# Softmax of short key rows: the mask added by TensorE, one maximum per PSUM bank, and one shared ring for the loads of q, k and v

## The chip, the cores and the metric

The kernel runs on one core of a Trainium2 chip. The metric is the device time of one execution in microseconds (us). A core has TensorE (PE, matmuls; its weight loads are listed as PEld), VectorE (DVE), ScalarE (ACT), GpSimd (POOL) and a queue engine, SyncE (SP), that here issues nearly all transfers; each engine takes its instructions in the order written.

## The reference

Three stages. First, causal attention with a memory term for B=4 batches, H=8 heads, S=576 positions, D=64 (float32):

```python
scores = scale * np.matmul(q, k.transpose(0, 1, 3, 2))
scores = np.where(causal, -1000000000.0, scores)
scores = scores - scores.max(-1, keepdims=True)
a = np.exp(scores)
a /= a.sum(-1, keepdims=True) + 1e-09
local = np.matmul(a, v)
...
return (g * mem_out + (1 - g) * local).astype(np.float32)
```

`mem_out` is `phi(q) @ M_prev` divided by `phi(q) @ z_prev`. Its output, 2304 tokens of 512 values, goes through two feed-forward layers 512 -> 2048 -> 512, the first with softplus, the second with squared ReLU. All eight weight and activation products are wanted at float32 precision, so the kernel splits each operand in a high and a low 16-bit part and uses three matmuls for one.

## The kernel before

The 4 x 576 query rows are cut into 18 chunks of 128 rows: for two batches at a time, chunk 0 of both, chunk 1 of both, and so on, then one chunk made of the last 64 rows of both. A chunk sees `EXT` keys: 128, 256, 384, 512 or 640. Eight of the 18 chunks (four of 128 keys, four of 256) are the short ones, and they come at two places: chunks 0 to 3 at the very start, chunks 9 to 12 in the middle (their scores fall at about 280 to 350 us).

A step of attention (`emit_s`) takes one head, or for the short chunks a group of `G` heads (4 of 128 keys, 2 of 256), so that a step always has 512 key columns there. For each head TensorE writes the scores into one of two PSUM banks (`s_ps[:, h % 2]`), DVE runs one pass over them (line 314: add the mask, scale, write to `p` in SBUF, and accumulate the minimum into `cs`), and ACT takes the exponential from SBUF with that minimum as bias (line 318). `emit_p` then splits the probabilities in two 16-bit parts (ACT line 330, DVE line 331), and a DMA transpose, or TensorE in the first two chunks, turns them for `emit_pv`.

The inputs of a chunk are loaded by `load` into float32 tiles: `rawk`, `rawq` and `rawv` have one buffer each in the pool `att`; `k` of chunk 1 has one more in the pool `stage`. `prep_k` (lines 226, 227), `prep_q` (217 to 220), `prep_v` (234, 235) and `prep_phi` (251 to 257) turn them into 16-bit parts on ACT and DVE. A `rawq` is read by `prep_q` and later by `prep_phi`, and only then is its buffer free for the next chunk's q. Up to nine chunks of prepared keys and values (`KVB = 9`) are kept.

Work of the first feed-forward layer is laid between the steps of attention: `unit_h` (lines 434 to 436, PSUM tile `hps`), `unit_xq` (496 to 498, `xacc`) and `unit_x` (451 to 453, `xps`). Its 32 weight pieces `wst`, 512 KB each, come as int64-packed words through three staging buffers and are converted by `split_piece`: DVE lines 417, 418, 419 and 422, ACT line 421. The first `unit_h` needs the attention output `xn` of chunks 0 and 1 (line 386), since a block has 256 tokens. The order on each engine is made ahead of time by a list scheduler with priorities (`tc.high_priority`); the second layer (lines 717 to 834) comes after all attention.

Of the kernel before, what the change touches and what calls it, by code (L numbers as in the profile page):

```python
# [8 lines left out]
F32 = mybir.dt.float32  # L9
F16 = mybir.dt.float16  # L10
BF16 = mybir.dt.bfloat16
I32 = mybir.dt.int32
I64 = mybir.dt.int64
AF = mybir.ActivationFunctionType
ALU = mybir.AluOpType
AX = mybir.AxisListType

P = 128
# [20 lines left out]
NST = 3  # L39
PTB = 4  # L40
PB = 2
P16 = 2
ST2 = 4

# [2 lines left out]
def kernel(  # L47
# [15 lines left out]
    pe, act, dve, pool, sp = nc.tensor, nc.scalar, nc.vector, nc.gpsimd, nc.sync  # L63
    B, H, S, D = q.shape
# [46 lines left out]
    att = att_cm.__enter__()  # L111
# [4 lines left out]
    stage = stage_cm.__enter__()  # L116


    mask = att.tile([P, 2, 4 * P], BF16, name="mask")
# [15 lines left out]

    p16 = [att.tile([P, 2 * EMAX], F16, name=f"p16_{i}") for i in range(P16)]
    zero = stage.tile([P, P], F16, name="zero", bufs=1)
    ident = stage.tile([P, P], F16, name="ident", bufs=1)
    make_identity(nc, ident)
    dve.memset(zero, 0.0)  # L140
    for t in p16:
        dve.memset(t, 0.0)
    s_ps = sps.tile([P, 2, 512], F32, name="s_ps")
# [16 lines left out]
    raw, qT, phiT, KT, V, Mt, Pt, PT, pvt, cs_t = ({} for _ in range(10))  # L160

    def segs(g):
        x = CH[g]
        if len(x) == 2:
            return [(x[0], P * x[1], 0, P)]
        return [(2 * x[0] + i, 4 * P, i * R, R) for i in range(2)]

    def lo_eng(g):
        return dve if g < LOE else pool

    def load(nm, g, pool_=None):
        if g >= NC or (nm, g) in raw:
            return
        src = {"q": q, "k": k, "v": v}[nm]
        t = (pool_ or att).tile([P, H, D], F32, name="raw" + nm, bufs=1)
        for b, s0, r0, n in segs(g):
            sp.dma_start(out=t[r0:r0 + n], in_=src[b, :, s0:s0 + n, :].rearrange("h p d -> p h d"))
        raw[nm, g] = t
    def load_m(g):
        for b, s0, r0, n in (segs(g) if g < NC else []):  # L180
            if s0 == 0:
                t = att.tile([P, EMAX], F32, tag="Pt", name="mraw", bufs=PB)[:, :HD].rearrange("p (h d) -> p h d", h=H)
                for i in range(2):
# [3 lines left out]
    def transp(g, out, in_, lim):  # L187
        nblk = in_.shape[1] // P
        if g >= lim:
            step = nblk if nblk <= 12 else nblk // 2  # L190
            for a in range(0, nblk, step):
                e = a + step
                sp.dma_start_transpose(out=out[:, a:e], in_=in_[:, a * P:e * P])
            return
        for a in range(0, nblk, 8):
            e = min(nblk, a + 8)
            ps = mm.tile([P, 8, P], F16, tag="mm", name="tps")
            for i in range(a, e):
                pe.transpose(ps[:, i - a], in_[:, i * P:(i + 1) * P], ident)
            act.activation(out[:, a:e], ps[:, :e - a], AF.Copy)  # L200
# [47 lines left out]
    def prep_phi(g):  # L248
        r = raw.pop(("q", g))
        e = att.tile([P, H, D], F32, tag="prod", name="phie")  # L250
        act.activation(e, r, AF.Relu, scale=-1.0)
        act.activation(e, e, AF.Exp, scale=-1.0)
        f = att.tile([P, H, D], F32, name="phi")
        dve.scalar_tensor_tensor(f, r, 0.0, e, ALU.max, ALU.add)
        fn = att.tile([P, H, 2, D], F16, name="phin")
        act.activation(fn[:, :, 0, :], f, AF.Copy)
        lo_eng(g).tensor_tensor(fn[:, :, 1, :], f, fn[:, :, 0, :], ALU.subtract)
        phiT[g] = att.tile([P, H, P], F16, name="phiT", bufs=2)
        transp(g, phiT[g], fn.rearrange("p h t d -> p (h t d)"), TP)
# [18 lines left out]
    def kblocks(g):  # L278
        x = CH[g]
        if len(x) == 2:  # L280
            return [[POS[x[0], i]] for i in range(x[1] + 1)]
        return [[POS[2 * x[0] + j, i] for j in range(2)] for i in range(4)] + [[g]]

    def emit_s(g, h0):
        G, ext = GRP[g], EXT[g]
        p = att.tile([P, EMAX], F32, name="Pt", bufs=PB)
        if h0 == 0:
            cs_t[g] = att.tile([P, 2, H], F32, name="cs", bufs=3)
        cs = cs_t[g]
        mk = mask[:, :, :EMAX // 2] if ext > 512 else mask[:, 0, 4 * P - ext:]  # L290
        for i in range(G):
            h = h0 + i
            pf = p[:, i * ext:(i + 1) * ext]
            if ext <= 512:
                half = ext
                view, pw, mw = s_ps[:, h % 2, :ext], pf, mk
            else:
                half = ext // 2
                view = s_ps[:, :, :half]
                pw, mw = pf.rearrange("p (a c) -> p a c", a=2), mk  # L300
            for j, ks in enumerate(kblocks(g)):
                a, n = j * P, P // len(ks)
                while a < (j + 1) * P:
                    e = min((j + 1) * P, (a // half + 1) * half)
                    bank = a // half if half < ext else h % 2
                    o = s_ps[:, bank, a % half:a % half + e - a]
                    for t in range(2):
                        for x, kb in enumerate(ks):
                            pe.matmul(  # L309
                                o[x * n:(x + 1) * n], qT[g][:, t * H + h, x * n:(x + 1) * n],  # L310
                                KT[kb][:, h, a - j * P:e - j * P], start=(t == 0), stop=(t == 1),
                            )
                    a = e
            dve.tensor_tensor_reduce(  # L314
                out=pw, in0=view, in1=mw, scale=-0.125, scalar=3.0e38,
                op0=ALU.add, op1=ALU.min, accum_out=cs[:, 0, h:h + 1],
            )
            act.activation(  # L318
                pf, pf, AF.Exp, bias=cs[:, 0, h:h + 1], scale=-1.0, accum_out=cs[:, 1, h:h + 1],
            )  # L320
        Pt[g, h0] = p
# [185 lines left out]


    load("k", 0)
    load("q", 0)  # L510
    load("k", 1, stage)
    load("v", 0)
    gates()
    z_setup()
# [5 lines left out]
    def prep_part(g, part):  # L520
        if g >= NC:
            return
        if part == 0:
            prep_k(g)
            load("k", g + 1)
        elif part == 1:
            prep_q(g)
        elif part == 2:
            prep_phi(g)
            load("q", g + 1)  # L530
        elif part == 3:
            prep_v(g)
            load("v", g + 1)
            prep_m(g)
            load_m(g + 1)

    prep_k(0)
    prep_q(0)
    prep_phi(0)
    load("q", 1)  # L540
    prep_v(0)
# [13 lines left out]
    def attn_step(s):  # L555
        if s < len(steps):
            g, h = steps[s]
            G = GRP[g]
            with tc.high_priority(HS):
                emit_s(g, h)  # L560
            nst = H // G
            i = h // G
            for part in range(4):
                if part * nst // 4 == i:
                    prep_part(g + 1, part)
            with tc.high_priority(HP):
                emit_p(g, h)
        for g, h0 in pv_at.get(s, ()):
            for h in range(h0, h0 + GRP[g]):
                with tc.high_priority(HV):  # L570
                    emit_pv(g, h)
                if h % 4 == 3:
                    with tc.high_priority(HXE):
                        emit_x(g, h // 4)
# [311 lines left out]
```

## Time and profile before

| | us |
|---|---|
| median of three runs (all: 976.44, 976.58, 980.92) | 976.58 |
| the profiled execution, its own time | 977.68 |
| span of the profiled execution | 975.9 |
| time around the span (977.68 less 975.9) | 1.78 |

The span is from the first to the last instruction of the core. A row of the profile that names `L314` speaks of line 314 of the kernel; `out<-in` are the program's tile names. Busy shares are of the stretch named; the granted clock (PEclk) is 1.00 at 2.4 GHz and 0.50 at 1.2 GHz.

### The profile page before, as it was taken

To read this page: it belongs to the slowest core of one execution; us is meant where nothing else is said; L and a number is where in the kernel's file an instruction comes from. 1 tells how busy PE (TensorE), PEld (TensorE's weight loads), DVE (VectorE), ACT (ScalarE), POOL (GpSimd) and SP (SyncE) were. 2 spreads that over 40 slices of the span, in tenths; PEclk is the share of its full clock that TensorE was granted. 3 is DMA by queue.
4 is the path that set the end of the run, shared out by engine and by line. 5 is a ranking of instruction groups with operands and counts; after the bars stand their busy time and mean duration, and the time that the engine had idled before them with its cause. 6 is when DMAs were issued, how large, how long until landed. Compare 5 with 4: busy or idle time off the path is not lost.

```text
span 975.9 us, 21791 instructions
## 1 busy us (share of the span) xinstructions
PE 884.2 (91%) x8994; PEld 680.1 (70%) x9012; DVE 668.0 (68%) x1437; ACT 587.2 (60%) x1094; POOL 2.2 (0%) x10
## 2 busy tenths in 40 slices
PE   4345898889998899999999999999999999999998
PEld 3234787778877788888888888544684585486483
DVE  7998998877748677675846499998894075066050
ACT  7765878768649687775937556562274065056051
POOL 0000000000000000000000000000000000000000
PEclk8555999999999999999999999999999999999999
DMA  9999989755699976646554375620000000000000
GB/s 232 224 241 215 214 162 195 118 95 112 99 159 176 160 125 104 104 83 108 94 88 80 64 234 172 211 65 22 22 2 11 33 1 4 30 12 1 33 12 22
DMA packets 283219, 101.05 MB, mean 104 GB/s; under 512 B 248048, under 2 KB 280816, under 8 KB 283120
## 3 DMA queue, kind: packets, MB, share of 16 engines
q1 hardware_dynamic: 282880, 99.65, 51.3%
q8 instruction: 70, 1.15, 0.5%
q14 instruction: 29, 0.24, 0.1%
q10 hardware_dynamic: 240, 0.02, 0.0%
HBM read 48.78 MB, written 4.72 MB: 55 GB/s over the span
## 4 chain that ended last, share of the span: by engine, by line
PE 60%; DMA 16%; DVE 13%; ACT 6%; issue 3%; SPq 1%; ACTq 0%; DVEq 0%
DMA PT<-p 8%; PE ops L829 7%; PE ops L827 6%; PE ops L828 6%; PE h2ps L801 4%; PE h2ps L799 4%; PE h2ps L800 4%; DMA rawq<-in_q_dram 3%; PE xps L452 3%; PE xps L451 3%; PE xps L453 3%; PE s_ps L309 3%; PE pvt L354 2%; PE hps L436 2%; PE hps L435 2%
## 5 line engine op out<-in xcount | busy, mean ns | idle before, releaser
L434 PE MATMUL hps<-x,W 128*128 128x256 f16 x576 | 157.8, 276 | 3.2 <-DVE cc L273 3.0
L435 PE MATMUL hps<-x,W 128*128 128x256 f16 x576 | 158.4, 276 | 1.7 <-ACT x L477 1.7
L436 PE MATMUL hps<-x,W 128*128 128x256 f16 x576 | 158.2, 275 | 0.0
L452 PE MATMUL xps<-g,W 128*128 128x256 f16 x512 | 138.5, 273 | 1.7 <-DVE g L445 1.7
L453 PE MATMUL xps<-g,W 128*128 128x256 f16 x512 | 138.7, 273 | 0.0
L451 PE MATMUL xps<-g,W 128*128 128x256 f16 x512 | 137.5, 273 | 1.1 <-DVE spa L441 0.7
L318 ACT ACTIVATE Pt<-Pt,cs 128x128 f32<-128x128 f32 (+4 forms) x144 | 84.2, 585 | 67.4 <-DVE cs L314 67.4
L309 PE MATMUL s_ps<-KT,qT 128*128 128x128 f16 (+2 forms) x992 | 83.9, 225 | 36.6 <-DVE cs L314 35.9
L829 PE MATMUL ops<-W,gg 128*128 128x512 f16 x288 | 108.5, 379 | 0.9
L827 PE MATMUL ops<-W,gg 128*128 128x512 f16 x288 | 109.2, 379 | 0.1
L828 PE MATMUL ops<-W,gg 128*128 128x512 bf16 x270 | 102.3, 379 | 0.0
L309 PEld LDWEIGHTS <-qT 128*128 128x128 f16 (+1 forms) x992 | 59.8, 105 | 48.5 <-issue 43.7
L331 DVE TENSOR_TENSOR p<-Pt,p 128x512 f16<-128x512 f32 (+2 forms) x104 | 69.3, 667 | 29.6 <-ACT p L330 28.8
L831 ACT ACTIVATE osb<-ops 128x512 f32<-128x512 f32 x18 | 10.8, 597 | 123.4 <-PE ops L829 123.4
L808 DVE TENSOR_TENSOR r<-h2ps,r 128x512 f32<-128x512 f32 (+1 forms) x16 | 10.0, 623 | 108.0 <-PE h2ps L801 107.2
L354 PE MATMUL pvt<-V,PT 128*128 128x64 f16 (+1 forms) x1392 | 60.7, 197 | 19.5 <-DMA PT<-p 18.3
L314 DVE CUSTOM_DVE_ANT_0 Pt<-s_ps,mask 128x128 f32<-128x128 f32 (+3 forms) x128 | 62.0, 485 | 18.6 <-PE s_ps L309 17.9
L354 PEld LDWEIGHTS <-PT 128*128 128x128 f16 (+1 forms) x1392 | 50.3, 104 | 28.7 <-DMA PT<-p 25.1
L330 ACT ACTIVATE p<-Pt 128x512 f16<-128x512 f32 (+2 forms) x104 | 63.1, 606 | 11.2 <-DMA PT<-p 10.2
L435 PEld LDWEIGHTS <-W 128*128 128x128 f16 x576 | 56.9, 99 | 10.2 <-issue 3.6
L799 PE MATMUL h2ps<-XT,WS 128*128 128x256 f16 (+1 forms) x256 | 63.7, 259 | 0.0
L800 PE MATMUL h2ps<-XT,WS 128*128 128x256 f16 (+1 forms) x256 | 63.7, 259 | 0.0
(160 smaller groups left out, 2076.5 us busy)
## 6 DMA issues: line engine op xcount, KB each, us to landing
wst<-in_moe_w_in_dram SPq DMA_DIRECT2D x32, 512.0 KB, 5.0
wst<-in_moe_w_out_dram SPq DMA_DIRECT2D x32, 512.0 KB, 4.7
rawk<-in_k_dram SPq DMA_DIRECT2D x16, 256.0 KB, 4.3
rawq<-in_q_dram SPq DMA_DIRECT2D x16, 256.0 KB, 3.9
rawv<-in_v_dram SPq DMA_DIRECT2D x16, 256.0 KB, 4.7
out_dram<-osb SPq DMA_DIRECT2D x16, 256.0 KB, 2.0
PT<-p SPq DMA_TRANSPOSE x100, 3.4
mraw<-in_M_prev_dram SPq DMA_DIRECT2D x8, 128.0 KB, 3.7
```

Of the source, the lines that this page charges most:

```text
L309: pe.matmul(o[x * n:(x + 1) * n], qT[g][:, t * H + h, x * n:(x + 1) * n], KT[kb][:, h, a - j * P:e - j * P], start=(t == 0), stop=(t == 1),)
L354: pe.matmul(o[r], t[:, o0 + i + y, r], V[kb][:, z, h, :], start=(i == 0 and y + z == 0), stop=(i == nb - 1 and y > 0),)
L434: pe.matmul(o, wh, x[:, c], start=(c == 0), stop=False)
L435: pe.matmul(o, wh, x[:, NCC + c], start=False, stop=False)
L436: pe.matmul(o, wl, x[:, c], start=False, stop=(c == NCC - 1))
L451: pe.matmul(ps, wh, gh, start=(f == f0), stop=False)
L452: pe.matmul(ps, wh, gl, start=False, stop=False)
L453: pe.matmul(ps, wl, gh, start=False, stop=(f == f1 - 1))
L799: pe.matmul(o, wh, xh, start=(k == 0), stop=False)
L827: pe.matmul(ps, gh, W4[0][:, f, :], start=(a == 0), stop=False)
L828: pe.matmul(ps, gh, W4[1][:, f, :], start=False, stop=False)
L829: pe.matmul(ps, gl, W4[0][:, f, :], start=False, stop=(a == NFC - 1))
```

## The change

For chunks of up to 256 keys a step now takes one of the two PSUM banks for all its heads (`sb`, the bank alternating by step). TensorE adds the mask of the diagonal block by one more matmul a head (identity `idb` as weights, the 128 x 128 mask as moving operand), DVE takes the maximum over all heads of the bank with one `tensor_reduce` and scales it with a small `tensor_scalar`, and ACT takes each head's exponential from PSUM. Chunks of more keys run the same code as before. Beside it, the loads of q, k and v share one tag of `RAWB = 2` buffers in place of one buffer each (and one in `stage`), and `phi` is computed in place.

```diff
--- before.py
+++ after.py
@@ -39,6 +39,7 @@
 NST = 3
 PTB = 4
 PB = 2
+RAWB = 2
 P16 = 2
 ST2 = 4
 
@@ -138,6 +139,8 @@
     ident = stage.tile([P, P], F16, name="ident", bufs=1)
     make_identity(nc, ident)
     dve.memset(zero, 0.0)
+    idb = att.tile([P, P], BF16, name="idb")
+    act.activation(idb, ident, AF.Copy)
     for t in p16:
         dve.memset(t, 0.0)
     s_ps = sps.tile([P, 2, 512], F32, name="s_ps")
@@ -168,11 +171,11 @@
     def lo_eng(g):
         return dve if g < LOE else pool
 
-    def load(nm, g, pool_=None):
+    def load(nm, g):
         if g >= NC or (nm, g) in raw:
             return
         src = {"q": q, "k": k, "v": v}[nm]
-        t = (pool_ or att).tile([P, H, D], F32, name="raw" + nm, bufs=1)
+        t = att.tile([P, H, D], F32, tag="raw", name="raw" + nm, bufs=RAWB)
         for b, s0, r0, n in segs(g):
             sp.dma_start(out=t[r0:r0 + n], in_=src[b, :, s0:s0 + n, :].rearrange("h p d -> p h d"))
         raw[nm, g] = t
@@ -250,7 +253,7 @@
         e = att.tile([P, H, D], F32, tag="prod", name="phie")
         act.activation(e, r, AF.Relu, scale=-1.0)
         act.activation(e, e, AF.Exp, scale=-1.0)
-        f = att.tile([P, H, D], F32, name="phi")
+        f = e
         dve.scalar_tensor_tensor(f, r, 0.0, e, ALU.max, ALU.add)
         fn = att.tile([P, H, 2, D], F16, name="phin")
         act.activation(fn[:, :, 0, :], f, AF.Copy)
@@ -287,6 +290,28 @@
         if h0 == 0:
             cs_t[g] = att.tile([P, 2, H], F32, name="cs", bufs=3)
         cs = cs_t[g]
+        if G > 1:
+            sb = s_ps[:, h0 // G % 2].rearrange("p (g e) -> p g e", g=G)
+            for i in range(G):
+                h = h0 + i
+                for j, (kb,) in enumerate(kblocks(g)):
+                    o = sb[:, i, j * P:(j + 1) * P]
+                    last = (j + 1) * P == ext
+                    for t in range(2):
+                        pe.matmul(o, qT[g][:, t * H + h], KT[kb][:, h], start=(t == 0), stop=(t == 1 and not last))
+                    if last:
+                        pe.matmul(o, idb, mask[:, 0, 3 * P:], start=False, stop=True)
+            hs = slice(h0, h0 + G)
+            dve.tensor_reduce(cs[:, 0, hs], sb, AX.X, ALU.max)
+            dve.tensor_scalar(cs[:, 0, hs], cs[:, 0, hs], -0.125, None, ALU.mult)
+            for i in range(G):
+                h = h0 + i
+                act.activation(
+                    p[:, i * ext:(i + 1) * ext], sb[:, i], AF.Exp,
+                    bias=cs[:, 0, h:h + 1], scale=0.125, accum_out=cs[:, 1, h:h + 1],
+                )
+            Pt[g, h0] = p
+            return
         mk = mask[:, :, :EMAX // 2] if ext > 512 else mask[:, 0, 4 * P - ext:]
         for i in range(G):
             h = h0 + i
@@ -508,7 +533,7 @@
 
     load("k", 0)
     load("q", 0)
-    load("k", 1, stage)
+    load("k", 1)
     load("v", 0)
     gates()
     z_setup()
```

The scheduler makes a new order of all of it. SP, from its second row, where `raw`, `mraw` and `wst` are the loads of inputs, of the memory matrix and of weight pieces. Before:

```order
L177 DMA rawk<-in_k_dram 128x8x64
L177 DMA rawq<-in_q_dram 128x8x64
L177 DMA rawk<-in_k_dram 128x8x64
L177 DMA rawv<-in_v_dram 128x8x64
L184 DMA mraw<-in_M_prev_dram 64x8x64 x2
L398 DMA wst<-in_moe_w_in_dram 128x4x128 x3
L184 DMA mraw<-in_M_prev_dram 64x8x64 x2
L177 DMA rawq<-in_q_dram 128x8x64
L177 DMA rawk<-in_k_dram 128x8x64
L177 DMA rawv<-in_v_dram 128x8x64
L398 DMA wst<-in_moe_w_in_dram 128x4x128
L401 DMA wst<-in_moe_w_out_dram 128x4x128 x2
```

And now, on the same engine from the same place:

```order
L180 DMA rawk<-in_k_dram 128x8x64
L180 DMA rawq<-in_q_dram 128x8x64
L187 DMA mraw<-in_M_prev_dram 64x8x64 x2
L423 DMA wst<-in_moe_w_in_dram 128x4x128 x3
L180 DMA rawk<-in_k_dram 128x8x64
L187 DMA mraw<-in_M_prev_dram 64x8x64 x2
L180 DMA rawv<-in_v_dram 128x8x64
L423 DMA wst<-in_moe_w_in_dram 128x4x128
L426 DMA wst<-in_moe_w_out_dram 128x4x128
L180 DMA rawq<-in_q_dram 128x8x64
L426 DMA wst<-in_moe_w_out_dram 128x4x128
L180 DMA rawv<-in_v_dram 128x8x64
```

The second k, the first v and what follows moved behind weight pieces; over the first 59 DMA rows the queue issued 18 weight pieces before and issues 23 now.

TensorE, in the scores of chunk 0 (`KT` the keys, `qT` the queries, turned). Before, one matmul of the scores stands here, between transposes (`tps`) and ahead of the first products with the memory matrix:

```order
L199 LDWEIGHTS kn
L199 MATMUL tps<-ident,kn 128x128
L309 LDWEIGHTS qT
L309 MATMUL s_ps<-KT,qT 128x128
L346 LDWEIGHTS phiT
L346 MATMUL pvt<-Mt,phiT 128x64
```

Now the rest of the first step's four heads stands there, each with its mask; its last heads and what follows are:

```order
L301 LDWEIGHTS qT
L301 MATMUL s_ps<-KT,qT 128x128
L301 LDWEIGHTS qT
L301 MATMUL s_ps<-KT,qT 128x128
L303 LDWEIGHTS idb
L303 MATMUL s_ps<-mask,idb 128x128
L371 LDWEIGHTS phiT
L371 MATMUL pvt<-Mt,phiT 128x64
```

What moved is the rhythm of the scores: before, TensorE had at most two heads ahead of DVE; now it writes a whole step of four heads, and then the next step into the other bank.

## Rows read from the trace of the kernel before

**Rows 1.** The page: busy time of TensorE, and slices of a fortieth each.

```profile
PE 884.2 (91%) x8994; PEld 680.1 (70%) x9012; DVE 668.0 (68%) x1437; ACT 587.2 (60%) x1094; POOL 2.2 (0%) x10
...
PEclk8555999999999999999999999999999999999999
```

**Rows 2.** Windows: length, busy of PE, PEld, DVE, ACT, POOL; clock, DMA share, GB/s.

```profile
25.00:50.00 25.00, 9.30 (x84) 6.49 (x84) 23.21 (x65) 19.24 (x47) 0.00 (x0) 0.50 1.11 231
50.00:75.00 25.00, 9.79 (x115) 7.82 (x113) 24.30 (x72) 16.23 (x38) 0.00 (x0) 0.50 1.15 245
...
87.50:200.00 112.50, 99.29 (x1180) 86.70 (x1181) 99.77 (x243) 83.95 (x173) 0.00 (x0) 0.94 0.90 173
...
187.50:200.00 12.50, 8.45 (x93) 6.92 (x92) 7.95 (x22) 8.84 (x19) 0.00 (x0) 0.86 0.79 138
...
275.00:350.00 75.00, 67.30 (x823) 59.18 (x821) 51.80 (x144) 52.59 (x121) 0.00 (x0) 1.00 1.05 172
350.00:560.00 210.00, 202.85 (x2708) 178.79 (x2706) 134.94 (x324) 148.92 (x307) 0.00 (x0) 1.00 0.53 91
560.00:975.00 415.00, 408.44 (x2861) 267.12 (x2876) 249.43 (x396) 184.41 (x250) 0.00 (x0) 1.00 0.17 53
```

**Rows 3.** Waits, 0 to 125 us: total, times, longest, in us.

```profile
PE s_ps L309 <- DVE cs L314: 32.1, 21, 3.8
```

**Rows 4.** Timeline of DVE: two chunks' mask passes and what starts behind them.

```profile
14.81 0.28 DVE L314 CUSTOM_DVE_ANT_0 Pt<-s_ps,mask 128x128 f32<-128x128 f32 x1
...
15.02 0.69 DVE L418 SCALAR_TENSOR_TENSOR wcv<-wst,wcv 128x512 int32<-128x512 int32 x1
15.62 0.28 DVE L314 CUSTOM_DVE_ANT_0 Pt<-s_ps,mask 128x128 f32<-128x128 f32 x1
...
53.51 0.42 DVE L314 CUSTOM_DVE_ANT_0 Pt<-s_ps,mask 128x256 f32<-128x256 f32 x1
...
53.85 0.20 DVE L274 RECIPROCAL cc<-cc 128x8 f32<-128x8 f32 x1
...
54.07 0.40 DVE L417 TENSOR_SCALAR wcv<-wst 128x512 int32<-128x512 int32 x1
54.38 0.68 DVE L331 TENSOR_TENSOR p<-Pt,p 128x512 f16<-128x512 f32 x1
```

**Rows 5.** Timeline of PE: six score matmuls between products of the feed-forward layer.

```profile
132.79 0.50 PE L309 MATMUL s_ps<-KT,qT 128*128 128x128 f16 x6
133.13 0.27 PE L435 MATMUL hps<-x,W 128*128 128x256 f16 x1
```

**Rows 6.** Timeline of DVE, then PE: output of chunk 1, first product of the layer.

```profile
86.73 0.68 DVE L386 TENSOR_TENSOR xn<-xf,xn 128x512 f16<-128x512 f32 x1
...
89.68 0.42 PE L434 MATMUL hps<-x,W 128*128 128x256 f16 x1
```

**Rows 7.** DMA issues, 0 to 125 us: count, size, median us to landing.

```profile
rawk<-in_k_dram SPq DMA_DIRECT2D x10, 256.0 KB, 4.6
rawq<-in_q_dram SPq DMA_DIRECT2D x6, 256.0 KB, 5.5
```

**Rows 8.** The chain, 130 to 205 us: start, us, what.

```profile
143.01 6.28 DMA wst<-in_moe_w_in_dram
...
187.66 0.61 DVE phi L254
...
189.41 2.50 DMA rawq<-in_q_dram
...
193.57 0.64 ACT qn L217
```

**Rows 9.** Timeline of ACT, then PE: waits before two instructions.

```profile
99.11 0.63 ACT L226 ACTIVATE kn<-rawk 128x512 f16<-128x512 f32 x1 [2.38 <-DMA rawk<-in_k_dram]
...
195.29 0.38 PE L496 MATMUL xacc<-g,W 128*128 128x256 f16 x2 [1.98 <-ACT g L444]
```

**Rows 10.** Waits of PE, 275 to 350 us.

```profile
PE pvt L354 <- DMA PT<-p: 5.4, 4, 2.3
```

## Prediction, made before the changed kernel ran

> **What bounds the kernel now.** I read the page's busy line and slices first. TensorE is busy 91% of the span, but the first four slices are different: the granted clock is 1.2 GHz in three of them [rows 1]. The windows say what rules there: from 25 to 75 us DVE is busy 47.5 of 50 us, the DMA share is above 1, and TensorE has work for only 19 us [rows 2]. From 560 us on TensorE is busy 408.4 of 415 us, and 202.9 of 210 between 350 and 560: nothing shortens these stretches but less work for TensorE [rows 2]. So the span is the time until TensorE gets enough work (its first product of the feed-forward layer starts at 89.7 us, 3 us after DVE has finished chunk 1's output [rows 6]), plus its work from there on, plus its gaps: 13.2 us between 87.5 and 200, 7.7 us between 275 and 350 [rows 2]. The wait that looks worst, 32.1 us of TensorE for the mask passes in the first 125 us [rows 3], lies in the stretch where TensorE has little to do and DVE is full; taking it away is worth nothing by itself unless DVE gets ahead.
>
> **The change, part by part.** *DVE's passes.* A recorded duration (0.28 and 0.42 us [rows 4]) overstates what a pass takes from a full DVE, since the next instruction starts before the last has ended: behind a pass of 128 keys the next starts after 0.21 us, of 256 after 0.34 us, behind a 512-wide float32 pass after 0.60 us [rows 4]. A step of four heads of 128 costs 4 x 0.21 = 0.84 us, of two heads of 256 2 x 0.34 = 0.68 us. The trace has no `tensor_reduce`. Its bounds are 0.31 us, the 512-wide `tensor_scalar` of line 417, and 0.69 us, a 512-wide float32 instruction without any overlap [rows 4]; I take 0.60, since it too reads 512 float32 values one stream long, and 0.1 for the small scaling (the reciprocal of eight values and what stands with it: 0.22 us for three [rows 4]). A step then costs 0.70 us: a saving of 0.14 in 8 steps, a loss of 0.02 in 16. That is 0.8 us over the whole kernel (8.0 at the lower bound of the reduction, a loss of 1.3 at the upper): one instruction for many is not where a gain would come from.
>
> *What DVE does before the first product.* The order counts more. Up to chunk 1's output DVE had 9 k and 8 v preparations, 10 splits of probabilities, and 16 passes of 128 keys and 13 of 256; now 6 k, 5 v, 8 splits and 9 reductions with scaling. The short ring of load buffers holds the far-ahead keys back. Six preparations and two splits at 0.60 are 4.8 us less; the passes are 16 x 0.21 + 13 x 0.34 = 7.8 against 9 x 0.70 = 6.3, 1.5 less; weight conversions moved forward cost two of line 417, two 418/419 and one 422, 2 x 0.31 + 3 x 0.60 = 2.4 more. Sum: -3.9 us.
>
> *The ring.* Before, q, k and v each had a buffer; now three streams share two. A load takes 4.6 to 5.5 us to land [rows 7] and its preparation some 1.3 us (two instructions, one on ACT and one on DVE), so a buffer turns round in about 7 us at best, and with 2 to 3 us of queueing in 9 to 10. A chunk needs three loads: 1.5 turns of the two buffers, 14 to 15 us, where the first four chunks ran at some 20 us each (chunk 1's output was done at 86.7 [rows 6]). Room, but not much: following the early loads by hand (k1 at 12 us, q1 at 22, k2 at 31, v2 at 39, q3 at 46) each is 0 to 2 us later than DVE reaches its preparation. Priced at +2 us (0 to +8).
>
> *Weights earlier, far keys later.* Over the first 59 transfers 23 weight pieces are issued in place of 18, so products that waited for weights get them sooner. In the trace such a piece is on the chain at 143 us for 6.3 us, and at 99 us ACT's queue stood 2.4 us for a key load nine chunks ahead [rows 8, 9]. Part of it was covered by other products of TensorE: -2 us (0 to -6).
>
> *q no longer behind phi.* Before, the next q could only be loaded once `phi` had read the last. At 187.7 us that is the chain: phi, q's load, then ACT's conversion at 193.6 [rows 8]; ACT's queue stands, its `g` behind it comes late, and TensorE waits [rows 9]. In the new order the eighth `qn` of DVE (row 315) stands ahead of the seventh `phi` (row 341; before 387 and 370). TensorE was idle for 4.0 of the 12.5 us from 187.5 on and its clock fell to 0.86 [rows 2], part of the 13.2: -3 us (0 to -4).
>
> *The masks.* 64 more matmuls of 128 columns. Six such take 133.13 - 132.79 = 0.34 us at full clock [rows 5], 57 ns each. Those of chunks 0 to 3 fall where TensorE idles; the 32 of chunks 9 to 12 fall where it is busy 67.3 of 75 us [rows 2]: +1.8 us, the cover being gone there.
>
> *The second place of short chunks, 275 to 350 us.* Prepared keys and values of eight chunks are loaded in a heap; the DMA share is 1.05 [rows 2], and TensorE waits 5.4 us for transposed probabilities [rows 10]. The ring spreads these loads to some 450 us. I take -2 us (-5 to +4, where the ring itself makes a q or k late).
>
> The exponential from PSUM adds nothing to DVE; a bank is held until ACT has read it, but two banks alternate and a step has other work between. Trainium skill, "Trainium Kernel Development and Optimization", section Best Practices: double-buffer, so that transfers overlap compute. That speaks against two buffers for three streams. By that rule the loads of the first chunks come into view; the trace's 4.6 to 5.5 us a load set the size, which is the rival below.
>
> Sum: -3.9 + 2 - 2 - 3 + 1.8 - 2 = -7.1 us against the profiled execution: span 968.8, time 970.6. It lay 1.1 us above the median of the runs shown, so the forecast for a median is 969.5 us.
>
> **The rivals.** *The ring makes loads late (slower).* One mechanism: q, k or v of a chunk arrives after its consumer stands at the head of ACT's or DVE's queue, and everything behind it waits. For it: DVE is full, the transfers are full, three streams on two buffers; q is held from its load to `phi`, so at times one buffer serves all else. Against: fewer bytes are asked for in the first 90 us, and a chunk has 20 us for 15. It decides from about 1.5 us a load on: some eight loads up to chunk 3 late by 1.5 us each are 12 us, and with the -3.9 and the masks that gives 976.6 - 3.9 + 1.8 + 12 = 986 us or so, 980 to 992.
>
> *Nothing comes of it.* DVE's start gains 3.9, the ring takes it back, TensorE's gaps later only move, the masks cost 1.8: 975 to 979. For it: the passes save 0.8 us, and TensorE is the bound from 90 us on.
>
> *More than forecast.* The gaps between 90 and 200 us (13.2) mostly close, since weights, q and the start all come sooner: 976.6 - 3.9 - 9 + 1.8 = 965, less with the second place: 958 to 964.
>
> **How the numbers follow.** Forecast 0.55 (964 to 974), of which 0.45 below 971.7 and 0.10 above; nothing 0.21; ring late 0.18; more 0.06. A change of 0.5%, 4.9 us, is about what a measurement of this kernel can tell from none. Faster 0.45 + 0.06 = 0.51, same 0.10 + 0.21 = 0.31, slower 0.18. The range runs from 962 to 981; it leaves out most of the ring's case and half of the best, under 2 in 10.
>
> **What would show it.** Right: the first `hps` matmul at about 86 to 88 us in place of 89.7; a `tensor_reduce` of about 0.69 us whose successor starts 0.60 later; the last of the 32 weight conversions some 10 us before its old place; no stop of ACT at a q load between 185 and 200; DMA share under 1 from 275 to 350. Wrong: waits of ACT or DVE for `raw` loads between 20 and 90 us that grow beyond 8 us in sum, a first `hps` after 92 us, or gaps of TensorE between 275 and 350 above 10 us.

## The result, and the profile after

The changed kernel takes 991.57 us (median of four runs, 986.69 to 992.98) beside 978.02 us before (four runs): 1.0129 times as long, 95% interval 1.0094 to 1.0164. The forecast was 969.5, the range 962 to 981. It is slower by more than 0.5%.

The page of the changed kernel's profiled execution, busy time of TensorE and the granted clock by slices (beside [rows 1]):

```profile
span 991.2 us, 21856 instructions
...
PE 896.1 (90%) x9058; PEld 689.3 (70%) x9076; DVE 666.7 (67%) x1357; ACT 584.5 (59%) x1095; POOL 2.2 (0%) x10
...
PEclk9999999999999999999999999999999999999999
```

TensorE is "busy" 12 us longer, of which the 64 mask matmuls can be 3.6. DVE has 1.3 us less to do (668.0 in [rows 1]). In this execution TensorE had the full clock from the start, where [rows 1] has half of it in three slices; it has little to do there in both, and the early clock did not make the start: the changed order of e1 below starts its first product at 83.46 us with half the clock there, the old order of e11 at 90.06 us with the full one. The windows, columns as in [rows 2]:

```profile
87.50:200.00 112.50, 95.43 (x1168) 83.91 (x1165) 99.02 (x232) 85.65 (x182) 0.00 (x0) 0.98 0.85 168
187.50:200.00 12.50, 8.77 (x106) 7.18 (x104) 9.31 (x21) 9.06 (x20) 0.00 (x0) 0.86 0.92 166
275.00:350.00 75.00, 68.94 (x847) 60.42 (x846) 51.64 (x125) 53.86 (x130) 0.00 (x0) 0.95 0.99 164
350.00:560.00 210.00, 200.27 (x2539) 172.16 (x2537) 128.85 (x297) 143.05 (x292) 0.00 (x0) 0.98 0.53 91
560.00:975.00 415.00, 411.32 (x2969) 274.14 (x2985) 255.35 (x407) 187.91 (x258) 0.00 (x0) 1.00 0.18 53
```

Read the number of matmuls, not the busy time: from 350 to 560 us TensorE is busy almost as long as before (200.27 for 202.85 in [rows 2]) but does 2539 matmuls in place of 2708; the rest follows after 560 us. Much of the time went there. The start looks as forecast, and better. DVE (a maximum and what follows it; the scaling of that maximum and what follows it; the output of chunk 1; the last of the 32 weight conversions):

```profile
54.05 0.68 DVE L305 TENSOR_REDUCE cs<-s_ps 128x2 f32<-128x512 f32 x1
54.65 0.68 DVE L444 SCALAR_TENSOR_TENSOR wcv<-wst,wcv 128x512 int32<-128x512 int32 x1
...
56.79 0.16 DVE L306 TENSOR_SCALAR cs<-cs 128x2 f32<-128x2 f32 x1
56.86 0.42 DVE L442 TENSOR_SCALAR wcv<-wst 128x512 int32<-128x512 int32 x1
...
80.04 0.68 DVE L411 TENSOR_TENSOR xn<-xf,xn 128x512 f16<-128x512 f32 x1
...
167.86 0.68 DVE L447 TENSOR_TENSOR W<-wcv,W 128x512 bf16<-128x512 f32 x1
```

and TensorE's first product of the layer:

```profile
83.05 0.37 PE L459 MATMUL hps<-x,W 128*128 128x256 f16 x1 [0.60 <-ACT x L203]
```

Chunk 1's output is 6.7 us and the first product 6.6 us earlier than in [rows 6]. How the lead goes is seen on one instruction of each block of the layer, the low half of `g`, counted from the start of the layer. The 55th, 58th and 61st of 72, before:

```profile
485.70 0.69 DVE L445 TENSOR_TENSOR g<-spa,g 128x512 f16<-128x512 f32 x1
...
526.14 0.69 DVE L445 TENSOR_TENSOR g<-spa,g 128x512 f16<-128x512 f32 x1
...
542.61 0.69 DVE L445 TENSOR_TENSOR g<-spa,g 128x512 f16<-128x512 f32 x1 [1.39 <-ACT g L444]
```

and after:

```profile
488.37 0.68 DVE L470 TENSOR_TENSOR g<-spa,g 128x512 f16<-128x512 f32 x1
...
535.58 0.69 DVE L470 TENSOR_TENSOR g<-spa,g 128x512 f16<-128x512 f32 x1
...
556.07 0.69 DVE L470 TENSOR_TENSOR g<-spa,g 128x512 f16<-128x512 f32 x1 [1.90 <-ACT g L469]
```

At 488 us the changed kernel is 2.7 us behind, at 536 us 9.4, at 556 us 13.5, and at the 72nd 13.6 (602.23 and 615.85). So some 9 us were given away before 488 us (from 6.6 ahead to 2.7 behind; the 10th of them is still 6.6 ahead at 155 us, the 30th is 3.7 behind at 322 us) and 11 in the last chunk of attention. TensorE there, in the changed kernel (time, duration, line, array shape, moving operand, count):

```profile
525.56 0.28 PE L460 MATMUL hps<-x,W 128*128 128x256 f16 x1
525.77 0.22 PE L334 MATMUL s_ps<-KT,qT 128*64 128x64 f16 x1
525.92 0.28 PE L461 MATMUL hps<-x,W 128*128 128x256 f16 x1
526.13 0.22 PE L334 MATMUL s_ps<-KT,qT 128*64 128x64 f16 x1
```

The last chunk holds 64 rows each of two batches, so most of its scores use 64 columns of the array (128*64). Here each stands alone between two products of the full array (128*128). A pair takes 526.13 - 525.77 = 0.36 us. Before, fifteen scores stand in a block; the row counts thirteen of 64 columns and two of the full array together:

```profile
527.74 0.68 PE L309 MATMUL s_ps<-KT,qT 128*64 128x64 f16 x15
528.26 0.27 PE L434 MATMUL hps<-x,W 128*128 128x256 f16 x1
528.37 0.27 PE L435 MATMUL hps<-x,W 128*128 128x256 f16 x1
```

That is 0.52 us for fifteen, with one change of shape among them, and 0.11 a product: 0.14 us for a score and a product. Nothing waits in either view, and the profile counts all of it as busy. In the written order of TensorE the shape changes 122 times before and 146 times after; in the last chunk alone 58 times before and 96 after. One window more shows it at its worst, 83 matmuls in 10 us at a granted clock of 0.66:

```profile
540.00:550.00 10.00, 10.00 (x83) 6.25 (x83) 4.22 (x11) 3.58 (x7) 0.00 (x0) 0.66 0.18 34
```

### The profile page after: what moved, and what is told of

Its sections match the earlier page's. It is cut to its first block, busy times and chain, and to the rows that moved or that the text cites. A ratio compares the mean times of both kernels' runs of the same rounds, so it can differ in the third digit from the quotient of the medians.

```text
span 991.2 us, 21856 instructions
## 1 busy us (share of the span) xinstructions
PE 896.1 (90%) x9058; PEld 689.3 (70%) x9076; DVE 666.7 (67%) x1357; ACT 584.5 (59%) x1095; POOL 2.2 (0%) x10
## 4 chain that ended last, share of the span: by engine, by line
PE 56%; DMA 8%; DVE 4%; ACT 3%; issue 1%; SPq 0%; ACTq 0%; DVEq 0%
PE ops L854 7%; PE ops L852 6%; PE ops L853 6%; PE h2ps L826 4%; PE h2ps L824 4%; PE h2ps L825 4%; DMA PT<-p 4%; PE hps L460 3%; PE hps L461 3%; PE hps L459 3%; PE xps L478 3%; PE xps L477 3%; PE xps L476 3%; PE s_ps L334 2%; PE pvt L379 2%; DMA qT<-qn 1%
## 5 line engine op out<-in xcount | busy, mean ns | idle before, releaser
L477 PE MATMUL xps<-g,W 128*128 128x256 f16 x512 | 140.5, 276 | 2.7 <-DVE g L470 2.7
L476 PE MATMUL xps<-g,W 128*128 128x256 f16 x512 | 139.1, 277 | 2.8 <-ACT g L469 2.7
L478 PE MATMUL xps<-g,W 128*128 128x256 f16 x512 | 140.2, 277 | 0.0
L343 ACT ACTIVATE Pt<-Pt,cs 128x384 f32<-128x384 f32 (+2 forms) x80 | 55.4, 693 | 42.4 <-DVE cs L339 42.1
L826 PE MATMUL h2ps<-XT,WS 128*128 128x256 f16 (+1 forms) x256 | 63.7, 259 | 0.0
L825 PE MATMUL h2ps<-XT,WS 128*128 128x256 f16 (+1 forms) x256 | 63.7, 259 | 0.0
L824 PE MATMUL h2ps<-XT,WS 128*128 128x256 f16 (+1 forms) x256 | 63.7, 259 | 0.0
L334 PE MATMUL s_ps<-KT,qT 128*128 128x128 f16 (+2 forms) x800 | 62.4, 219 | 1.4 <-DVE cs L339 1.4
L461 PEld LDWEIGHTS <-W 128*128 128x128 bf16 x576 | 57.0, 99 | 7.4
```

What stands on the lines that cost most here:

```text
L461: pe.matmul(o, wl, x[:, c], start=False, stop=(c == NCC - 1))
L476: pe.matmul(ps, wh, gh, start=(f == f0), stop=False)
L477: pe.matmul(ps, wh, gl, start=False, stop=False)
L478: pe.matmul(ps, wl, gh, start=False, stop=(f == f1 - 1))
L824: pe.matmul(o, wh, xh, start=(k == 0), stop=False)
L825: pe.matmul(o, wh, xl, start=False, stop=False)
```

## The experiments

Theory A: the loss is in the order that the scheduler made for the last chunk, where each change of array shape costs TensorE about 0.12 us. Rival B: the ring of two buffers makes loads and what is queued behind them late. Rival C: the short steps themselves cost. The ratios below are to the kernel before, run beside each; 0.1% is 1 us.

**e1, the last chunk in blocks.**

```diff
-            with tc.high_priority(HS):
+            with tc.high_priority(150 if g == NC - 1 else HS):
                 emit_s(g, h)
```

> The changed kernel, with the score matmuls of the last chunk alone (64 rows of each of two batches) at a higher priority, so that they stand in blocks and not one by one between full products; TensorE's order is the same up to that chunk, and 90 changes between 64-column and full array shapes stand in it in place of 146. Theory A (each change of shape costs TensorE about 0.12 us, 5 of the 13 us lost): 56 x 0.12 = 6.7 us less, 983 to 987 us. Rival B (the loss is waiting for loads and transposes through the shared ring; the alternation only fills time that would be waited anyway): 989 to 993 us.

981.52 us, 1.0039 (1.0023 to 1.0056), beside 1.0129: 9 to 10 us came back, more than A expected. TensorE in the last chunk:

```profile
521.96 0.85 PE L334 MATMUL s_ps<-KT,qT 128*64 128x128 f16 x22
522.64 0.27 PE L460 MATMUL hps<-x,W 128*128 128x256 f16 x1
```

All 22 scores of a head, twenty of 64 columns and two of the full array, take 0.68 us together. And the window that answers to the last one above:

```profile
540.00:550.00 10.00, 9.93 (x178) 8.20 (x177) 7.42 (x15) 8.38 (x16) 0.00 (x0) 1.00 0.49 92
```

178 matmuls in place of 83 (not the same ones, since e1 is ahead by then), and the clock does not fall. The traces give the parts. From the 55th low half of `g` to the 72nd the changed kernel takes 127.5 us, e1 115.9: 11.6 less. The 56 changes at 0.11 us (e7) are 6.2 of them; the clock, at half from 507.8 to 511.2 and from 542.0 to 548.8 us in the changed kernel's trace and nowhere in this stretch of e1's, is 5.1. That the order brings the fallen clock is not shown: in e8 TensorE's order is that of the kernel before up to 668 us, yet its clock is at half from 531.6 to 538.4 us, where the kernel before keeps the full one. For the changes of shape A holds, and B does not for this part: what filled the pairs was not time that would have been waited anyway.

**e2, the short steps alone.** The change without these lines:

```diff
-RAWB = 2
...
-        t = att.tile([P, H, D], F32, tag="raw", name="raw" + nm, bufs=RAWB)
+        t = (pool_ or att).tile([P, H, D], F32, name="raw" + nm, bufs=1)
...
-    load("k", 1)
+    load("k", 1, stage)
```

> The kernel before with the mask on TensorE, one maximum per bank, the exponential from PSUM, and phi in place, but with the separate load buffers of before. If the ring (with the order that it forces) is the cause: 974 to 980 us, no wait of TensorE for transposed probabilities above 4 us in 87.5 to 200 us. If the short steps themselves (bank held until ACT has read it, mask matmuls) are the cause: 986 to 992 us.

983.29 us, 1.0047 (1.0023 to 1.0072): between the two expectations, a loss of 4 to 5 us without the ring. TensorE's wait for transposed probabilities from 87.5 to 200 us, 4 us at most if the ring were the cause, is 6.8, so the short steps bring that wait by themselves.

**e3, the ring alone.** On the kernel before:

```diff
+RAWB = 2
...
-        t = (pool_ or att).tile([P, H, D], F32, name="raw" + nm, bufs=1)
+        t = att.tile([P, H, D], F32, tag="raw", name="raw" + nm, bufs=RAWB)
...
-        f = att.tile([P, H, D], F32, name="phi")
+        f = e
...
-    load("k", 1, stage)
+    load("k", 1)
```

> The kernel before with the shared ring of two buffers and phi in place alone; mask passes as before. If the ring is the cause: 986 to 993 us, with the same alternation in the last chunk (148 changes of shape in TensorE's order) and TensorE idle about 18 us in 87.5 to 200. If the short steps are the cause: 976 to 980 us.

986.25 us, 1.0080 (1.0053 to 1.0106), as the ring's theory has it at its lower edge. In the written order the last chunk is matmul for matmul that of the changed kernel, so it is the ring that brought the alternation (with `phi` in place, which is part of this edit and of e2's, and which no run has alone). The 0.8% here and the 0.5% of e2 make up the 1.3% of the whole change. The 18 us of idle time that I expected between 87.5 and 200 us are not there: TensorE is busy 101.11 of the 112.5 us, more than before.

```profile
87.50:200.00 112.50, 101.11 (x1217) 88.51 (x1216) 99.60 (x234) 85.02 (x177) 0.00 (x0) 0.95 0.89 170
```

**e4, four shared buffers.**

```diff
-RAWB = 2
+RAWB = 4
...
-    idb = att.tile([P, P], BF16, name="idb")
+    idb = mask[:, 1, EMAX // 2:EMAX // 2 + P]
```

> The changed kernel with four shared buffers in place of two (the identity moved into unused columns of the mask tile to make room). If two buffers are too few: the idle time of TensorE from 87.5 to 560 us falls back from 40 to 33 us or less and 114 changes of shape stand in its order in place of 146: 975 to 981 us. If the number of buffers does not matter (the merged order or the short steps cost): 987 to 993 us.

983.21 us, 1.0060 (1.0036 to 1.0085). Better than two buffers by some 7 us, but in neither expected range, and worse than three (e14); why a fourth buffer lost is open.

**e5 and e6, ring alone and short steps alone, each with the last chunk in blocks** (the edit of e1 on e3 and on e2).

> The ring alone (as e3) with the last chunk's scores in blocks (as e1): 92 changes of array shape in TensorE's order against 148 in e3. If the ring's whole loss comes from the order that it brings to the last chunk: 975 to 979 us, level with before or a little under it, since e3's trace is ahead of before's by some 6 us of TensorE work up to 350 us. If the ring costs by late loads as well: 981 us or more.

977.44 us, 0.9998 (0.9976 to 1.0019): all that the ring of two lost in e3 was the last chunk's order. From the 55th `g` to the 72nd it is 7.5 us shorter than e3, 6.2 by 56 changes and 1.7 by the clock, which in e3 is at half for 3.4 us there.

> The short steps alone (as e2, own load buffers) with the last chunk's scores in blocks: 106 changes of shape against 136 in e2. If e2's loss of 5 us is made of changes of shape (16 more than before late, some 2 us) and of mask matmuls (1.8 to 3.5 us): 978 to 981 us. If the short steps lose in some other way: 982 us or more, as e2.

981.46 us, 1.0032 (1.0016 to 1.0048), just above the first case. The short steps still lose some 3 us.

**e7 and e8, the price of a change of shape by itself**, where TensorE has no other stops. In `row_tile` of the kernel before:

```diff
+    def dummy(n):
+        for _ in range(n):
+            i = DUM[0] % 4
+            tc.keep_in_program_order(
+                pe.matmul(dps[:64, :128], W4[0][:, i, :64], W4[0][:, i, 128:256], start=True, stop=True))
...
+            if t0 == 0 and m < 3:                     # e7
+                dummy(1)
+            if t0 == 0 and m < 3 and a == NFC - 1:    # e8
+                dummy(NFC)
```

> The kernel before with 48 more matmuls of 64 columns of weights by 128 (nobody reads them) in the second layer's first three row tiles, where TensorE never waits: one behind every third full product. It has 90 changes of array shape more than e8. Theory A (a change of shape costs about 0.12 us even where nothing waits): 10 to 12 us longer than e8. Rival B (no price of the change itself): within 1 us of e8.

> The same 48 matmuls as in e7, in three blocks of 16 at the ends of the same three row tiles: 6 changes of shape in place of 96. Both theories: 1.5 to 3.5 us longer than the kernel before, for 48 matmuls of 0.03 to 0.06 us.

990.48 us (1.0121, 1.0076 to 1.0166) and 983.56 us (1.0050, 1.0022 to 1.0077). The medians lie 6.9 us apart (two and four runs), the spans of the two profiles, 991.9 and 982.0, 9.9 us: 0.08 to 0.11 us for each of the 90 changes. e8's own 5.5 us are more than its matmuls explain; both kernels also fix the order of all row tiles and leave the second layer one PSUM bank less, so only their difference is a price, and the rest of the program adds its own noise to it. The three row tiles themselves settle it: from the first product of the first to that of the fourth e7 takes 44.47 us (658.22 to 702.69), e8 34.42 (658.33 to 692.75), at the full clock in both. 10.05 us for 90 changes are 0.11 us each. The rows show how. e7, TensorE and its weight loads (PEld):

```profile
661.43 0.38 PE L840 MATMUL ops<-W,gg 128*128 128x512 f16 x1
661.74 0.11 PEld L828 LDWEIGHTS <-W 128*64 128x64 f16 x1 [0.42 <-issue]
661.74 0.24 PE L828 MATMUL dps<-W 128*64 128x128 f16 x1
661.91 0.10 PEld L838 LDWEIGHTS <-gg 128*128 128x128 f16 x1
661.91 0.39 PE L838 MATMUL ops<-W,gg 128*128 128x512 f16 x1
661.92 0.10 PEld L839 LDWEIGHTS <-gg 128*128 128x128 f16 x1
662.14 0.38 PE L839 MATMUL ops<-W,gg 128*128 128x512 bf16 x1
```

and e8:

```profile
668.26 0.38 PE L839 MATMUL ops<-W,gg 128*128 128x512 bf16 x1
668.48 0.38 PE L840 MATMUL ops<-W,gg 128*128 128x512 f16 x1
668.79 1.08 PE L828 MATMUL dps<-W 128*64 128x128 f16 x16
669.80 0.39 PE L838 MATMUL ops<-W,gg 128*128 128x512 f16 x1
```

A full product is followed by the next of its shape after 0.22 us (668.26 to 668.48), but by one of the other shape after 0.31 (668.48 to 668.79, 661.43 to 661.74): 0.09 us. Sixteen small ones take 1.01 us, about 0.06 each, but a single one between full ones 0.17: 0.11 us. The weight load goes with it: at a change it starts with its own matmul (661.74, 661.91), where otherwise it runs under the one before (661.92, for the matmul at 662.14). The Trainium skill, "TensorEngine Tiling (Array Packing)", section Tiling Modes, says that a change of the tiling mode, not of the tile alone, drains TensorE. It gives no price; these rows agree, with 0.09 to 0.11 us each way.

**e9 and e10, where the short steps lose.** On e6, e9 and then e10:

```diff
-                        pe.matmul(o, qT[g][:, t * H + h], KT[kb][:, h], start=(t == 0), stop=(t == 1 and not last))
-                    if last:
-                        pe.matmul(o, idb, mask[:, 0, 3 * P:], start=False, stop=True)
+                        pe.matmul(o, qT[g][:, t * H + h], KT[kb][:, h], start=(t == 0), stop=(t == 1))
```

```diff
-        if G > 1:
+        if G > 1 and g < 9:
```

> As e6 (short steps, own buffers, last chunk in blocks), with the 64 mask matmuls left out, so that the short chunks' rows see keys that they should not. 90 changes of shape stand in its order against 106 in e6, worth 1.8 us. If e6's remaining loss against before (3.3 us) is the mask matmuls (64 x 57 ns = 3.6 us, 1.8 of them in the busy second place): 976 to 978.5 us. If it is the form of the step (a bank held until ACT has read it): 979 to 982 us.

973.17 us, 0.9953 (0.9936 to 0.9971): 8 us under e6, more than the masks and the changes of shape together.

> As e6, with the short steps in their new form only at their first place (chunks 0 to 3); chunks 9 to 12 run the passes of before. 106 changes of shape as in e6. If the loss of e6 lies at the second place, where TensorE is busy and waits for the exponentials: 977.5 to 979.5 us, 2 to 3.5 less than e6. If it lies at the start: 980.5 to 982.5 us.

978.30 us, 1.0018 (0.9997 to 1.0039): by ratio 1.4 us under e6, within both intervals. Inconclusive.

**e11, the kernel before with the last chunk in blocks** (the edit of e1).

> The kernel before with the last chunk's scores in blocks, nothing else: 108 changes of shape in place of 122. At 0.11 us a change, as e7 and e8 gave it: 1.5 us less than before, 976 to 977.5 us. If the order of the last chunk matters only in the changed order: 978 us.

979.67 us, 1.0022 (0.9998 to 1.0047). A miss: 14 changes fewer did not show in the time. TensorE's order is that of the kernel before up to the last chunk, and there the trace is 1.2 us shorter (from the 55th `g` to the 72nd, 115.3 in place of 116.5), near the 1.5 expected; that is less than the interval can tell.

**e12 and e15, the ring of three alone, with blocks and without.** On e5 and on e3:

```diff
-RAWB = 2
+RAWB = 3
```

> A version meant to beat both kernels: the old mask passes, a ring of three buffers, phi in place, the last chunk's scores in blocks; 88 changes of shape against 122 before and 92 in e5. By the changes alone, 34 x 0.11 = 3.7 us less than before, 974 to 975 us; if what a ring gains at the start is again waited away between 275 and 350 us, with a fallen clock, as in e5: 976 to 978 us.

965.13 us, 0.9874 (0.9850 to 0.9898): faster than both kernels, by far more than the changes of shape account for.

> e12 without the blocks: old passes, three shared buffers, phi in place; 108 changes of shape against 88. At 0.11 us a change: 2.2 us more than e12, 967 to 968 us. If e12's gain came from the blocks: 975 us or more.

967.01 us, 0.9908 (0.9877 to 0.9939), as expected from e12. So the third buffer is the larger part, and e12 must be read against e5. Waits of ACT for input loads, 0 to 125 us (total, times, longest), in e5 with two buffers:

```profile
ACT V L235 <- DMA rawv<-in_v_dram: 6.9, 3, 4.2
...
ACT qn L218 <- DMA rawq<-in_q_dram: 6.4, 4, 3.5
ACT kn L227 <- DMA rawk<-in_k_dram: 5.1, 5, 1.6
...
ACT qn L208 <- DMA rawq<-in_q_dram: 0.9, 1, 0.9
```

and in e12 with three:

```profile
ACT kn L227 <- DMA rawk<-in_k_dram: 4.7, 5, 2.1
...
ACT V L235 <- DMA rawv<-in_v_dram: 1.9, 2, 0.9
...
ACT qn L208 <- DMA rawq<-in_q_dram: 0.7, 1, 0.7
```

19.3 us against 7.3. What follows, from 87.5 to 200 us, first e5, then e12:

```profile
87.50:200.00 112.50, 100.41 (x1209) 88.11 (x1208) 99.10 (x236) 84.88 (x176) 0.00 (x0) 0.95 0.88 170
```

```profile
87.50:200.00 112.50, 104.82 (x1295) 92.92 (x1294) 102.22 (x244) 87.01 (x181) 0.00 (x0) 0.97 0.89 172
```

86 matmuls more in the same time, with DVE, the busiest engine here beside TensorE, busier by 3 us. That the loads which come in time are the reason is argued, not shown: the changed kernel gains as much from the third buffer (e14), and there the same waits of ACT stay at 17.8 us with two buffers and 17.6 with three.

**e14 and e13, the changed kernel with three buffers, without and with blocks** (the same edit on the changed kernel and on e1).

> The changed kernel with three shared buffers in place of two and nothing else; 106 changes of shape. If the third buffer is what e12 had over e5 (12 us): e13 plus 18 x 0.11 = 2 us, and at least 15 us less than the changed kernel with two, 976 us or less. If the width of the ring matters only through the order of the last chunk: 991.6 less 40 changes at 0.11 to 0.18 us, 984 to 987 us.

974.72 us, 0.9977 (0.9954 to 1.0001): one more buffer takes 15 to 17 us off the changed kernel.

> The changed kernel with three shared buffers and the last chunk in blocks, that is e12 with the short steps in their new form; 88 changes of shape as in e12. If the short steps cost only their 64 mask matmuls (at most 3.6 us): 966 to 970 us. If they cost more by what they make late (as between e6 and e9, 8 us): 972 to 976 us. If they gain from DVE's saved passes: under 965 us.

973.46 us, 0.9972 (0.9949 to 0.9995). The blocks gave nothing measurable here, and the short steps cost 8 to 10 us against e12. From the 55th `g` to the 72nd the other pairs with and without blocks differ by 2.6 us for 30 changes (e2, e6), 2.1 for 20 (e15, e12) and 0.3 for 18 (e14, e13); at 0.11 us each they would be 3.3, 2.2 and 2.0.

**e16 and e17, mask matmuls left out of e13 and issued twice.**

> e13 with the 64 mask matmuls left out, so that the short chunks' rows see keys that they should not. If the price of the short steps is the mask matmuls' own time (64 x 57 ns, at most 3.6 us): 969 to 973 us. If it is the masks and what they make late, as e9 was 8 us under e6: 963 to 967 us. If it is the rest of the step (one maximum, the exponential from PSUM) or the order made for it: 972 to 975 us, as e13.

976.13 us, 0.9973 (0.9953 to 0.9993), by ratio the same as e13.

> e13 with each of the 64 mask matmuls issued twice (the mask is added twice to the scores). If the masks' own time is the price: 974 to 977.5 us, up to 3.6 more than e13. If a mask matmul is hidden: within 1 us of e13, 972.5 to 974.5 us.

995.45 us, 1.0164 (1.0123 to 1.0205). Leaving 64 matmuls out changes nothing, and 64 more, worth 3.6 us, cost 19. So on this ring the masks' own time is not the price. Between the traces of e13 and e17 (27.8 us) TensorE starts the layer 5.6 us later, is idle 11.2 us more from there on and loses 7.7 us more to the half clock: each program has an order of its own, and with it more moves than the edit.

**e18, the scaling on ACT.** On e13:

```diff
-            dve.tensor_scalar(cs[:, 0, hs], cs[:, 0, hs], -0.125, None, ALU.mult)
+            act.activation(cs[:, 0, hs], cs[:, 0, hs], AF.Copy, scale=-0.125)
```

> e13 (short steps, ring of three, last chunk in blocks) with the small scaling of the maximum on ACT, right ahead of the exponentials that need it, so that nothing stands between the maximum and them on DVE. In the changed kernel's trace the scaling starts 2.1 us behind the maximum in the mean of 20 steps. If that wait is the price of the short steps: 965 to 969 us, near e12. If the order of the whole program is: 972 to 976 us, as e13.

977.72 us, 1.0001 (0.9980 to 1.0021). The long way from the maximum to its scaling (54.05 to 56.79 in the rows above) is real, but taking it out of DVE's queue gained nothing.

## Why the prediction was wrong, step by step

*The step that failed.* "Nothing shortens these stretches but less work for TensorE", said of 350 us on, took busy for useful. The two views that I read there, busy share and gaps, cannot show a change of order between matmuls of two shapes, and my sum had no term behind 350 us. The order of the last chunk cost 9 to 10 us against blocks (e1), some 6 by changes of shape at 0.11 us. Against the kernel before, the trace has 11 us more there: 4.2 by 38 changes more, 5.1 by the half clock, which no run ties to the order, and 1.4 by gaps. e3 and e5 show that the ring brought this order, not the short steps.

The terms ahead of 350 us failed too: they were to add to the lead of the start, and 10 us went between the 10th and the 30th block of the layer (155 to 322 us). Behind the first product TensorE's gaps sum to 47.7 us, before to 39.2, and half of the time spent at half the clock is 13.0 us in place of 6.2. With 6.6 us won at the start, 24 changes more (2.6) and some 2 us of masks behind the first product, an estimate from these rows, that is 13.3 of the 15.3 us by which the two spans differ.

*The ring, +2 us (0 to +8).* For late loads, which is what the term priced, the range held: with the last chunk in blocks the ring of two is level with the kernel before (e5). Alone it lost 8 us (e3), by the order of the last chunk, which the term left out. What the sum could not see is how much one more buffer gives: by ratio 15 to 17 us without blocks (e14 against the changed kernel, e15 against e3) and 7 to 12 with them (e13 against e1, e12 against e5). The 14 to 15 us of turns against the 20 of a chunk are averages and say nothing of it; which wait the third buffer takes away stays open (e12, e14).

*DVE's work before the first product, -3.9 us.* Right in direction, and too small: the first product came 6.6 us earlier, for 2 to 4 forecast. The ring alone brings 2.7 of it (87.03 us in e3), the short steps alone 4.8 (84.92 in e2), so that the new form was the larger part. *Weights earlier, -2.* The last conversion came 16.5 us earlier, at 167.86 us; before it was

```profile
184.36 0.68 DVE L422 TENSOR_TENSOR W<-wcv,W 128x512 bf16<-128x512 f32 x1
```

That is more than the 10 forecast, but TensorE had 95.43 us of work from 87.5 to 200 in place of 99.29: its gaps grew from 13.2 to 17.1 us. The weights are not to blame: with the ring alone (e3) the conversions ended at 172.7 us and TensorE had 101.11 us of work there. It is the new form that waits, for transposed probabilities. Before:

```profile
PE pvt L354 <- DMA PT<-p: 3.0, 3, 1.2
```

and after:

```profile
PE pvt L379 <- DMA PT<-p: 9.8, 9, 2.4
```

*q no longer behind phi, -3.* Did not come. ACT no longer stands for q there, but for v, and TensorE is idle for 3.7 of the 12.5 us as it was for 4.0:

```profile
193.43 0.63 ACT L237 ACTIVATE V<-rawv 128x512 f16<-128x512 f32 x1 [1.76 <-DMA rawv<-in_v_dram]
```

*The second place, -2.* The gaps fell from 7.7 to 6.1 us and the DMA share from 1.05 to 0.99, as forecast, but the clock fell to 0.95 in the mean where it had been 1.00, and that is some 3.4 of 75 us.

*DVE's passes, -0.8.* Right: 1.3 us less busy. The maximum takes 0.68 us, its successor starts 0.60 later (54.05 to 54.65), and the scaling holds DVE for 0.07. (The term's bounds were a gain of 7.8 and a loss of 1.4 us, not 8.0 and 1.3.)

*The masks, +1.8.* Not settled. The new form of the short steps was slower in all six pairs that differ by it (and, with own buffers, by phi in place), though most of the intervals are 0.2 to 0.3% to either side. By ratio: on the ring of two 0.5% (changed kernel, e3) and 0.4% with blocks (e1, e5), with own buffers 0.5% (e2) and 0.1% (e6, e11), on the ring of three 0.7% (e14, e15) and 1.0% (e13, e12). In all six pairs TensorE's wait for transposed probabilities from 87.5 to 200 us is longer with the new form (5.4 to 9.8 us, without it 2.9 to 7.5), and without masks it is 5.9 (e9) and 8.5 (e16), so this part is not the masks'. How much of the time is the matmuls' own, the form of the step, or the order made around them stays open: e9 speaks for the masks, e16 against, e18 against the wait for the scaling, and e17 shows a swing of 19 us for 3.6 us of work.

*The rivals.* "The ring makes loads late" had the number nearest (986 us, 980 to 992) and the right part of the change, but in the changed kernel not its mechanism: ACT's waits for loads between 20 and 90 us, my sign for it, are

```profile
ACT kn L229 <- DMA rawk<-in_k_dram: 5.3, 3, 2.8
ACT qn L220 <- DMA rawq<-in_q_dram: 3.2, 3, 1.6
ACT V L237 <- DMA rawv<-in_v_dram: 3.1, 2, 2.7
```

11.6 us in sum, where before they were 10.7 already; the bound of 8 that I named was passed before the change. What the ring of two cost, it cost through the order of the last chunk (e3, e5).

## What to carry to other kernels

Where a scheduler writes the order, a local change is a change of the whole program: compare the written order of the busiest engine from end to end, and in the trace count instructions per window, since busy time hides what lies between two matmuls. Keep matmuls that use a part of the array in blocks. Before taking buffers away, try one more: here a shared ring of three was the gain and the new form of the short steps the loss, and e12, three shared buffers with the old passes and the last chunk in blocks, beats both kernels at 965.13 us.

## What the runs showed of the hardware that was not expected

A change between 128*64 and 128*128 costs 0.09 to 0.11 us in each direction (e7), several times what a 64-column score of 128*64 itself takes in a block (0.52 us for fifteen scores and one change). The granted clock fell to 0.66 between 540 and 550 us of the changed kernel, that is to half for 6.8 us, though TensorE waited for nothing there; at 526 us, with the same pairs, the windows show 1.00, and e8 falls to half for 6.8 us in an order in which the kernel before does not. What sets that difference no run here tells.
